# A fused long convolution and cosine-gated MLP: work at the changes of stage moved forward in the queues, and half of one stage's matrices made by ScalarE and GpSimd

## The chip, the cores and the metric

The kernel runs on one core of a Trainium2 chip. The core has five queues that matter here, each of which works strictly in its own order: TensorE (PE, matrix products; its weight loads are shown as PEld), VectorE (DVE), ScalarE (ACT), GpSimd (POOL), and SyncE (SP), which here issues all DMA transfers. They wait for each other by semaphores. The metric is the device time of one execution in microseconds (us); the number compared is the median of several executions. All data are 32-bit floats, and every matrix product is made in two passes over TensorE.

## What is computed

```python
def _attn_ref(x, v, pos_emb, w1, w2):            # x, v: (4, 12480, 128)
    B, S, D = x.shape
    h_mlp = np.maximum(pos_emb @ w1, 0.0) @ w2
    window = np.exp(-0.01 * np.arange(S, dtype=np.float32))[:, None]
    h_filt = h_mlp * window
    u = x * v
    L = 2 * S
    Uf = np.fft.rfft(u, n=L, axis=1)
    Hf = np.fft.rfft(h_filt, n=L, axis=0)
    y = np.fft.irfft(Uf * Hf[None, :, :], n=L, axis=1)[:, :S, :]
    return x * y

def _moe_ref(x, w_in, w_out):                    # x: (49920, 128), w_in: (128, 2048)
    h = x @ w_in
    return (h * np.cos(h)) @ w_out
```

Each of the 128 channels of x*v, in each of 4 batches, is convolved with a long filter that a small network makes from the positions; the product with x goes, row by row, through an MLP of width 2048 whose gate is a cosine. The MLP's weights arrive as 64-bit floats and are turned into 32-bit ones on the chip.

## The kernel before, in words

The convolution is done by a Fourier transform in two factors, N1 = 96 and N2 = 120, all by matrix products, in four steps for each batch:

- **First step** (f1_units, L576): for each of 64 columns of channels two products with the table c1 (f1_mm, L404). A bank of PSUM holds a column's result, and either ScalarE or VectorE copies it to SBUF (f1_evict, L417 to L424; f1_takers at L408 deals the columns out by a share).
- **Second step** (f2_both_units, L604, for batch 0): 48 pairs of frequencies. Each frequency needs a matrix w of 124x120 (make_w, L299, by turn, L282): a sine table times one number plus another times another. Each pair takes two products with the signal (L445) and two with the filter (L448; from the middle on as four at L451). ScalarE copies the filter's result to a tile h (L624), SP stores h to DRAM (hd, L626) and w to DRAM (wd, L613), since batches 1 to 3 load both again (f2_units, L585). VectorE multiplies signal and h (f2_product, L464), GpSimd adds the two halves (L471).
- **Third step** (i1_units, L631): again 64 columns, products with the table cs (i1_mm, L476), a copy of one half by ScalarE (L484), sum and difference by VectorE (L486).
- **Fourth step** (i2_units, L659): 30 groups; each group takes four matrices of cosines (a tile tm, made by make_group, L642, or loaded from td) and products with them (i2_mm, L501); VectorE multiplies by x (zs, L506).

The order is written out by hand. Every step is a Python generator; each yield is a place where another generator may put its instructions, and what is emitted first stands first in its engine's queue. The helper `units(n, steps, before, mm, after, parts, ahead)` (L524) is the frame of all steps: `before(j)` prepares unit j and is called `ahead` units early, `mm` emits the products, and `after(j)` takes the results out, one unit late.

For batch 0 the stages follow one another: the filter's network, the filter's first step (into ftile), batch 0's first step, second, third. While the filter's first step runs, GpSimd makes the remaining tables (inverse_tables, L252): every fifth yield advances them (L860 to L864), the sines themselves are taken by ScalarE (L226) up to four tables late, and what is left is emitted at once at the end. Into the first and the third step `beside` (L870) puts one piece of the conversion of w_in and w_out at every 14th yield (convert_units, L167: VectorE L133, L141, L151, GpSimd L135, L137, L147, L156, ScalarE L144 sig and L146 low), and in the third step, at every fifth of the others, one piece of the cosine matrices of six groups (some_groups, L653, through make_t, L305: two ScalarE instructions and one sum by GpSimd, L297). After them some_groups opens the fourth step of batch 0 (`next(backs[0])`, L657), which prepares its first group.

In the second step a matrix is made by one ScalarE multiplication into a bank of PSUM (L291) and one VectorE multiply-add (L293), one pair ahead and one being made; tiles w have two buffers, h three, t (L457) two. From the fourth step of batch 0 on, the convolution of the batches and the MLP (moe_up L734, moe_act L749, moe_down L756) are interleaved by counted steps, to the end.

Of the kernel before, what the change touches and what calls it, by code (L numbers as in the profile page):

```python
# [2 lines left out]

# [6 lines left out]
F32 = mybir.dt.float32  # L10
U32 = mybir.dt.uint32
AF = mybir.ActivationFunctionType
# [18 lines left out]
def kernel(  # L31
# [46 lines left out]
    nc = tc.nc  # L78
# [4 lines left out]
    N1, N2 = 96, 120  # L83
    R = S // N2
    M = N1 * N2
# [3 lines left out]
    KE = ODD + H  # L89
# [5 lines left out]
    CB = D // 2  # L95
# [156 lines left out]
    def inverse_tables(pool):  # L252

        t = Tables(pool, nc.gpsimd, 4)
        part = t.whole([P, 1], [[1, 1]], channel_multiplier=1, name="part")
        part4 = t.whole([P, 1], [[1, 1]], base=1, channel_multiplier=4, name="part4")
        step = t.whole([P, P], [[1, P]], name="step")
        mid = t.whole([P, P], [[1, P]], base=-MID, name="mid")
        cs, (rows, tw_t) = third_table(pool), last_tables(pool)
        yield from t.sines(step, part, N2, [(cs[:, 0, 0:H + 1], 1), (cs[:, 1, 0:H + 1], 0)],  # L260
                           eighths=slice(0, H + 1, H))
        yield from t.sines(step[:, 1:H], part, N2,
                           [(cs[:, 0, H + 1:], 0), (cs[:, 1, H + 1:], 1)])
        yield from t.sines(step, part4, 4 * N1,
                           [(rows[:, i, :], q) for i, q in enumerate((0, 1, 2, 3))])
        yield from t.sines(mid, part4, TURN, [(tw_t[:, 0, :], 1), (tw_t[:, 1, :], 0)],
                           eighths=slice(H - 1, N2, H))
        t.finish(len(t.waiting))
        for kept, made in ((csd, cs), (rowsd, rows), (twd, tw_t)):
            nc.sync.dma_start(kept[:, :, :], made[:, :, :])  # L270

# [27 lines left out]
    def make_w(w, k1, **how):  # L299


        turn(w, even[:, 0, :], even[:, 1, :], tw_w[:, 0, k1:k1 + 1], tw_w[:, 1, k1:k1 + 1],
             **how)
# [146 lines left out]
            for r, src in enumerate((ftile[0:KE, :, k, :], above[0:KE, :, k - KF, :])):  # L450
                nc.tensor.matmul(pi[:, r], w[:, i, :], src, start=True, stop=True)  # L451

    def f2_product(pool, ps, h, k1, whole):


        y = parts[0:N2, :, k1:k1 + 2, :, :].rearrange("p r k b i -> p r b (k i)")
        t = pool.tile([N2, 2, CB, 4], F32, name="t", bufs=1 + whole)  # L457
        uu = ps[0:N2, :].rearrange("p (r b j) -> p r b j", r=2, j=4)
        if whole:
            for r, (dst, hh) in enumerate(((y, h[:, :, :, :]), (t[:, :, :, :], h[:, ::-1, :, :]))):  # L460
                u = uu[:, r]
                twice = bass.AP(tensor=u.tensor, offset=u.offset,
                                ap=[u.ap[0], [0, 2], *u.ap[1:]])
                nc.vector.tensor_tensor(dst, twice, hh, op=ALU.mult)  # L464
                yield
        for r, op in ((0, ALU.subtract), (1, ALU.add)):
            if not whole:
                nc.vector.tensor_tensor(y[:, r], uu[:, 0], h[:, r], op=ALU.mult)
                yield
                nc.vector.tensor_tensor(t[:, r], uu[:, 1], h[:, 1 - r], op=ALU.mult)  # L470
            nc.gpsimd.tensor_tensor(y[:, r], y[:, r], t[:, r], op=op)  # L471
            yield

    def i1_mm(ps, b, i):
# [101 lines left out]
    def f1_units(bank, u, share=0.5, evict=f1_evict):  # L576
        def mm(j, ps, i):
            if i == 0:
                ps = bank()
            f1_mm(ps, u, j, i)  # L580
            return ps

        return units(CB, F1_STEPS, lambda j: None, mm, lambda j, ps: evict(ps, j, share), 2)
# [17 lines left out]
            yield from units(N1 // 2, F2_STEPS, before, mm,  # L601
                             lambda j, ps: f2_product(pool, ps, hs.pop(j), 2 * j, False), 4)

    def f2_both_units(bank):  # L604

        with tc.tile_pool(name="both", bufs=2) as pool:
            ws = {}

            def before(j):
                ws[j] = pool.tile([KE, 2, N2], F32, name="w")  # L610
                for i in range(2):
                    make_w(ws[j][:, i, :], 2 * j + i, half=bank)
                nc.sync.dma_start(wd[j, :, :, :], ws[j][:, :, :])  # L613

            def mm(j, ps, i):
                if i == 0:
                    ps = bank(), bank()
                for filt in range(2):
                    f2_mm(ps[filt], ws[j], 2 * j, i, filt=filt == 1)
                return ps  # L620

            def after(j, ps):
                h = pool.tile([N2, 2, CB, 4], F32, name="h", bufs=3)
                nc.scalar.activation(h[:, :, :, :].rearrange("p r b j -> p (r b j)"),  # L624
                                     ps[1][0:N2, :], AF.Copy, scale=1.0 / M)
                nc.sync.dma_start(hd[j, :, :, :, :], h[:, :, :, :])  # L626
                yield from f2_product(pool, ps[0], h, 2 * j, True)

            yield from units(N1 // 2, F2_STEPS, before, mm, after, 4, ahead=1)

    def i1_units(bank):  # L631
        with tc.tile_pool(name="mid", bufs=2) as pool:
# [20 lines left out]
    def some_groups(pool):  # L653
        for g in SOME:
            t = pool.tile([N1, G, 2, R], F32, name="some", bufs=2)
            yield from make_group(pool, g, t, G, bufs=2)
        next(backs[0])  # L657

    def i2_units(bank, b, bufs):  # L659

# [133 lines left out]
    with tc.manual_schedule():  # L794
        with tc.tile_pool(name="psum", bufs=8, space=PSUM) as psum, \
                ExitStack() as first:
            def bank():
                return psum.tile([P, BANK], F32, name="ps")
# [58 lines left out]
            keep.__exit__(None, None, None)  # L857
            with tc.tile_pool(name="tables", bufs=1) as pool:
                sines = inverse_tables(pool)
                for i, _ in enumerate(f1):  # L860
                    if i % 5 == 0:
                        next(sines, None)
                for _ in sines:
                    pass  # L864

            backs = [inverse_units(lambda: bank(), b) for b in range(B)]

            def beside(units, pieces, more=lambda pool: iter(())):  # L870
                with tc.tile_pool(name="convert", bufs=1) as pool:
                    convert, other = convert_units(pool, pieces), more(pool)
                    for i, _ in enumerate(units):
                        if i % 14 == 0:
                            next(convert, None)
                        elif i % 5 == 0:
                            next(other, None)
                    for _ in [*convert, *other]:
                        pass

            beside(f1_units(bank, slots[0:R, :, :, :], 0.55),
                   [(wind[:, c], w) for c, w in in_pieces])
            lpool = ctx.enter_context(tc.tile_pool(name="late", bufs=1))
            cs = third_table(lpool)
            nc.sync.dma_start(cs[:, :, :], csd[:, :, :])
            for _ in f2_both_units(bank):
                pass
            first.close()

# [97 lines left out]
```

## Time and profile before

| what | us |
|---|---|
| median of 7 executions | 3782.46 |
| lowest and highest | 3780.46 and 3784.91 |
| the profiled execution | 3780.46 |
| its span, first to last instruction | 3778.6 |
| TensorE busy | 3699.9 (98%) |
| VectorE busy | 2762.1 (73%) |
| GpSimd busy | 2590.5 (69%) |
| ScalarE busy | 2520.4 (67%) |
| mean granted TensorE clock | 0.994 |

Times in the profile count from the start of the span. A line of a stage table gives the stretch, its length, then for each engine its busy time and, in brackets, its number of instructions, then the granted clock of TensorE (1.00 is full), the busy share of the 16 DMA engines and GB/s. A line of waits names the waiting engine, tile and line, the one it waited for, and the time in total, how often and the longest. A line of the timeline gives start, duration, engine, line, operation, tiles (written <- read), shapes, how many instructions are merged, and in brackets the engine's idle time before and who ended it. SPq is SP's queue of DMA issues; the time shown is that of issuing, not of the transfer.

### The profile page before, as it was taken

What the parts mean: (1) busy time and instruction counts of PE and PEld (TensorE: products, weight loads), DVE (VectorE), ACT (ScalarE), POOL (GpSimd) and SP (SyncE); (2) the same over time, 40 slices, a digit from 0 to 9 for tenths busy, and PEclk for the clock granted to TensorE, in tenths of its full rate; (3) what the DMA queues carried; (4) which work ended last, traced back from release to release, by engine and by line L of the source; (5) the groups of instructions that cost most, each with busy time, mean ns of one, the idle gap of its engine ahead of it and who ended that gap; (6) DMA issues with size and microseconds to landing.
All of it is one profiled execution on the core that took longest, in us unless ns stands there. A gap on an engine that the chain in (4) does not pass through costs nothing.

```text
span 3778.6 us, 47199 instructions
## 1 busy us (share of the span) xinstructions
PE 3699.9 (98%) x13546; PEld 2108.4 (56%) x13546; DVE 2762.1 (73%) x5562; ACT 2520.4 (67%) x4683; POOL 2590.5 (69%) x2342
## 2 busy tenths in 40 slices
PE   7898999999999999999999999999999999999999
PEld 6777555655466555555565556555566544444444
DVE  7887887688866777778766786788765566666666
ACT  5757776766665557766655567666664677777777
POOL 7667886588854665688745664788644577777776
PEclk9899999999999999999999999999999999999999
DMA  6263441022202650122103540122105200000000
GB/s 166 67 181 109 149 148 54 19 72 78 74 18 68 181 156 27 35 76 79 57 18 111 176 123 21 48 79 75 41 12 168 87 22 18 17 21 19 17 22 13
DMA packets 209498, 276.14 MB, mean 73 GB/s; under 512 B 17111, under 2 KB 146535, under 8 KB 209111
## 3 DMA queue, kind: packets, MB, share of 16 engines
q1 hardware_dynamic: 209239, 273.12, 24.5%
q8 instruction: 109, 1.79, 0.2%
q14 instruction: 150, 1.23, 0.1%
HBM read 193.64 MB, written 79.42 MB: 72 GB/s over the span
## 4 chain that ended last, share of the span: by engine, by line
PE 83%; POOL 6%; DVE 3%; DMA 3%; ACT 2%; issue 2%; SPq 0%; POOLq 0%; DVEq 0%; ACTq 0%
PE ph L737 32%; PE acc L762 27%; PE cv L762 5%; PE cv L501 5%; PE cv L476 4%; POOL f L746 4%; PE cv L404 3%; PE cv L445 3%; PE ph L126 2%; DMA hd<-h 2%; PE ps L404 2%; DVE k L743 1%; ACT cs L751 1%; POOL tm L297 1%; PE ps L476 1%
## 5 line engine op out<-in xcount | busy, mean ns | idle before, releaser
L746 POOL TENSOR_TENSOR f<-a,k 128x512 f32<-128x512 f32 (+1 forms) x1568 | 1986.2, 1267 | 1050.5 <-DVE k L743 1050.2
L737 PE MATMUL ph<-at,w_in_sb 128*128 128x512 f32 (+1 forms) x3136 | 1599.0, 591 | 5.2 <-DVE gt L753 4.6
L740 ACT ACTIVATE a<-ph,quarter 128x512 f32<-128x512 f32 (+1 forms) x1568 | 1073.4, 685 | 756.6 <-PE ph L737 747.4
L762 PE MATMUL acc<-gt,w_out_sb 128*128 128x512 f32 (+1 forms) x2688 | 1374.3, 593 | 9.9 <-ACT ot L768 9.4
L753 DVE TENSOR_TENSOR gt<-ph,cs 128x512 f32<-128x512 f32 (+1 forms) x1568 | 1077.9, 687 | 317.7 <-ACT cs L751 289.3
L743 DVE TENSOR_SCALAR k<-a 128x512 f32<-128x512 f32 (+1 forms) x1568 | 769.9, 491 | 618.1 <-ACT a L740 601.7
L751 ACT ACTIVATE cs<-f 128x512 f32<-128x512 f32 (+1 forms) x1568 | 980.3, 625 | 330.3 <-POOL f L746 327.8
L762 PEld LDWEIGHTS acc<-gt,w_out_sb 128*128 128x128 f32 x2688 | 505.7, 189 | 662.7 <-issue 619.3
L737 PEld LDWEIGHTS ph<-at,w_in_sb 128*128 128x128 f32 x3136 | 553.6, 190 | 337.9 <-issue 264.6
L471 POOL TENSOR_TENSOR slots<-slots,t 120x256 f32<-120x256 f32 x384 | 311.1, 816 | 58.7 <-DVE t L464 26.2
L501 PEld LDWEIGHTS cv<-slots,tm 96*104 96x104 f32 x1920 | 240.1, 170 | 108.4 <-issue 80.7
L501 PE MATMUL cv<-slots,tm 96*104 96x128 f32 x1920 | 253.7, 274 | 9.7 <-DVE tm L293 4.9
L762 PE MATMUL cv<-gt,w_out_sb 128*128 128x512 f32 (+1 forms) x448 | 224.5, 583 | 0.7 <-DVE gt L753 0.7
L476 PEld LDWEIGHTS cv<-cs,slots 120*96 120x96 f32 x1536 | 176.7, 167 | 67.6 <-issue 65.7
L476 PE MATMUL cv<-cs,slots 120*96 120x120 f32 x1536 | 183.1, 266 | 0.0
L445 PE MATMUL cv<-slots,w 124*120 124x256 f32 x576 | 173.0, 380 | 0.0
L445 PEld LDWEIGHTS cv<-slots,w 124*120 124x120 f32 x576 | 103.6, 184 | 123.8 <-issue 111.1
L404 PEld LDWEIGHTS cv<-c,slots 104*124 104x124 f32 x768 | 132.5, 192 | 71.2 <-issue 58.3
L404 PE MATMUL cv<-c,slots 104*124 104x192 f32 x768 | 151.2, 326 | 4.8 <-DVE gt L753 3.5
L762 PEld LDWEIGHTS cv<-gt,w_out_sb 128*128 128x128 f32 x448 | 84.9, 190 | 104.5 <-issue 99.5
L392 DVE TENSOR_TENSOR xt<-xt,vt 104x256 f32<-104x256 f32 x177 | 138.1, 787 | 0.1
L486 DVE TENSOR_TENSOR slots<-cv,other 96x240 f32<-96x240 f32 x384 | 133.6, 394 | 4.2 <-ACT other L484 4.2
(129 smaller groups left out, 2565.5 us busy)
## 6 DMA issues: line engine op xcount, KB each, us to landing
h<-hd SPq DMA_DIRECT2D x144, 240.0 KB
tm<-td SPq DMA_DIRECT2D x96, 312.0 KB
xt<-in_x_dram SPq DMA_DIRECT2D x120, 208.0 KB
vt<-in_v_dram SPq DMA_DIRECT2D x120, 208.0 KB
xs<-in_x_dram SPq DMA_DIRECT2D x120, 208.0 KB
zd<-zs SPq DMA_DIRECT2D x119, 208.0 KB
zb<-zd SPq DMA_DIRECT2D x96, 256.0 KB
w<-wd SPq DMA_DIRECT2D x144, 116.2 KB
```

The costliest lines, as they stand in the source:

```text
L404: nc.tensor.matmul(ps[0:KE, i * 2 * N1:(i + 1) * 2 * N1], u[:, b, 0:KE, i], c1[0:u.shape[0], :, :].rearrange("p r k -> p (r k)"), start=Tr ...
L445: nc.tensor.matmul(pi, w[:, i, :], parts[0:KE, :, k], start=True, stop=True)
L471: nc.gpsimd.tensor_tensor(y[:, r], y[:, r], t[:, r], op=op)
L476: nc.tensor.matmul(ps[0:N1, (i * 2 + r) * N2:(i * 2 + r + 1) * N2], parts[0:N2, r, :, b, i], cs[:, r, :], start=True, stop=True)
L501: nc.tensor.matmul(ps[0:R, i * D:(i + 1) * D], t[:, i, r, :], slots[0:N1, :, place, :], start=(r == 0), stop=(r == 1))
L737: nc.tensor.matmul(ph[:, 0:m], w_in_sb[:, c * P:(c + 1) * P], ats[n][:, 0:m], start=True, stop=True)
L740: nc.scalar.activation(a[:, 0:m], ph[:, 0:m], AF.Identity, bias=quarter[:, 0:1], scale=INV_TWO_PI)
L743: nc.vector.tensor_scalar(out=k[:, 0:m], in0=a[:, 0:m], scalar1=ROUND, scalar2=ROUND, op0=ALU.add, op1=ALU.subtract)
L746: nc.gpsimd.tensor_tensor(f[:, 0:m], a[:, 0:m], k[:, 0:m], op=ALU.subtract)
L751: nc.scalar.activation(cs[:, 0:m], f[:, 0:m], AF.Sin, scale=TWO_PI)
L753: nc.vector.tensor_tensor(gt[:, 0:m], ph[:, 0:m], cs[:, 0:m], op=ALU.mult)
L762: nc.tensor.matmul(accs[n][:, 0:m], w_out_sb[:, c, :], gt[:, 0:m], start=(c == 0), stop=(c == NFC - 1))
```

## The change

It edits how batch 0's first three steps are put into the queues; the MLP part is untouched.

- inverse_tables yields between its last sines, and the generator that advances it goes on into batch 0's first step (`chain(f1, first_f1)`) instead of emitting the rest at once at the end of the filter's first step.
- f2_both_units prepares its first two pairs' matrices before batch 0's first step goes on (`next(f2)`), in buffers of their own (w_pool), and each later pair two ahead. Of a pair's two matrices the odd one is now made by ScalarE twice and a GpSimd sum (the `spare` way of turn, L295 to L297); the even one as before. Matrices have three buffers (two in w_pool, one in the step's pool), h has two. A pair's store wd is issued after the store hd of the pair before it in work, not when it is made.
- The last pair's two sums at the end of f2_product go to VectorE.
- `beside` puts conversions at every 11th yield in the first step and every 10th in the third, and the other work at yields 1, 5, 9 and so on.
- some_groups opens the fourth step before its last group, not after it.

```diff
         yield from t.sines(mid, part4, TURN, [(tw_t[:, 0, :], 1), (tw_t[:, 1, :], 0)],
                            eighths=slice(H - 1, N2, H))
-        t.finish(len(t.waiting))
+        while t.waiting:
+            t.finish(1)
+            yield
...
-    def f2_product(pool, ps, h, k1, whole):
+    def f2_product(pool, ps, h, k1, whole, sums=nc.gpsimd):
...
-            nc.gpsimd.tensor_tensor(y[:, r], y[:, r], t[:, r], op=op)
+            sums.tensor_tensor(y[:, r], y[:, r], t[:, r], op=op)
...
-    def f2_both_units(bank):
-
+    def f2_both_units(bank, w_pool):
+
+        ws, unkept = {}, []
+
+        def before(j):
+            ws[j] = (w_pool if j % 3 < 2 else pool).tile([KE, 2, N2], F32, name="w",
+                                                         bufs=2 if j % 3 < 2 else 1)
+            spare = (w_pool if j < 2 else pool).tile([KE, N2], F32, name="spare",
+                                                     bufs=1 if j < 2 else 2)
+            make_w(ws[j][:, 1, :], 2 * j + 1, spare=spare[:, :])
+            yield
+            make_w(ws[j][:, 0, :], 2 * j, half=bank)
+            unkept.append(j)
+            yield
+
+        def mm(j, ps, i):
+            if i == 0:
+                ps = bank(), bank()
+            for filt in range(2):
+                f2_mm(ps[filt], ws[j], 2 * j, i, filt=filt == 1)
+            return ps
+
+        def after(j, ps):
+            h = pool.tile([N2, 2, CB, 4], F32, name="h")
+            nc.scalar.activation(h[:, :, :, :].rearrange("p r b j -> p (r b j)"),
+                                 ps[1][0:N2, :], AF.Copy, scale=1.0 / M)
+            nc.sync.dma_start(hd[j, :, :, :, :], h[:, :, :, :])
+            while unkept:
+                k = unkept.pop(0)
+                nc.sync.dma_start(wd[k, :, :, :], ws[k][:, :, :])
+            yield from f2_product(pool, ps[0], h, 2 * j, True,
+                                  nc.vector if 2 * j + 2 == N1 else nc.gpsimd)
+
+        steps = units(N1 // 2, F2_STEPS, before, mm, after, 4)
+        yield next(steps)
         with tc.tile_pool(name="both", bufs=2) as pool:
-            ws = {}
-
-            def before(j):
-                ws[j] = pool.tile([KE, 2, N2], F32, name="w")
-                for i in range(2):
-                    make_w(ws[j][:, i, :], 2 * j + i, half=bank)
-                nc.sync.dma_start(wd[j, :, :, :], ws[j][:, :, :])
...
-                h = pool.tile([N2, 2, CB, 4], F32, name="h", bufs=3)
...
-            yield from units(N1 // 2, F2_STEPS, before, mm, after, 4, ahead=1)
+            yield from steps
...
             yield from make_group(pool, g, t, G, bufs=2)
-        next(backs[0])
+            if g == SOME[-2]:
+                next(backs[0])
...
-                for i, _ in enumerate(f1):
-                    if i % 5 == 0:
-                        next(sines, None)
-                for _ in sines:
-                    pass
+                first_f1 = f1_units(bank, slots[0:R, :, :, :], 0.55)
+                for i, _ in enumerate(chain(f1, first_f1)):
+                    if i % 5 == 0 and next(sines, "made") == "made":
+                        break
...
-            def beside(units, pieces, more=lambda pool: iter(())):
+            def beside(units, pieces, every, more=lambda pool: iter(())):
...
-                        if i % 14 == 0:
+                        if i % every == 0:
                             next(convert, None)
-                        elif i % 5 == 0:
+                        elif i % 4 == 1:
                             next(other, None)
...
-            beside(f1_units(bank, slots[0:R, :, :, :], 0.55),
-                   [(wind[:, c], w) for c, w in in_pieces])
+            w_pool = first.enter_context(tc.tile_pool(name="w", bufs=2, side="right"))
+            f2 = f2_both_units(bank, w_pool)
+            next(f2)
+            beside(first_f1, [(wind[:, c], w) for c, w in in_pieces], 11)
...
-            for _ in f2_both_units(bank):
+            for _ in f2:
                 pass
...
-            beside(i1_units(bank), [(w_out_sb[:, c, :], w) for c, w in out_pieces], some_groups)
+            beside(i1_units(bank), [(w_out_sb[:, c, :], w) for c, w in out_pieces], 10, some_groups)
```

More of the change, by code (lines that the diff above doesn't have):

```diff
@@ L2 @@
 from contextlib import ExitStack
+from itertools import chain
 import concourse.bass as bass
@@ L602, in f2_units @@
                              lambda j, ps: f2_product(pool, ps, hs.pop(j), 2 * j, False), 4)
-    def f2_both_units(bank):
-        with tc.tile_pool(name="both", bufs=2) as pool:
-            ws = {}
-            def before(j):
-                ws[j] = pool.tile([KE, 2, N2], F32, name="w")
-                for i in range(2):
-                    make_w(ws[j][:, i, :], 2 * j + i, half=bank)
[L613 to L622, printed above, removed]
-                h = pool.tile([N2, 2, CB, 4], F32, name="h", bufs=3)
[L624 to L627, printed above, removed]
-            yield from units(N1 // 2, F2_STEPS, before, mm, after, 4, ahead=1)
+    def f2_both_units(bank, w_pool):
[28 more added lines that the diff above has]
+        yield next(steps)
+        with tc.tile_pool(name="both", bufs=2) as pool:
+            yield from steps
```

## The prediction, made before the result was known

> **What bounds the kernel now.** I read the chain of work that ended last, then the whole span cut at the changes of stage, then who TensorE waits for. From the page:
>
> ```profile
> PE 83%; POOL 6%; DVE 3%; DMA 3%; ACT 2%; issue 2%; SPq 0%; POOLq 0%; DVEq 0%; ACTq 0%
> ```
>
> Stages cut where TensorE resumes (time, busy time of each engine, granted clock, DMA share, GB/s):
>
> ```profile
> 120.93:170.17 49.24, 44.38 (x252) 43.48 (x253) 40.35 (x110) 43.42 (x130) 29.45 (x32) 0.92 0.23 67
> 170.17:272.13 101.96, 96.57 (x483) 74.90 (x483) 85.56 (x191) 53.79 (x142) 68.00 (x96) 0.98 0.59 173
> 272.13:336.95 64.82, 55.58 (x510) 54.32 (x510) 50.08 (x155) 43.04 (x133) 44.58 (x58) 0.95 0.25 80
> 336.95:3778.60 3441.65, 3410.97 (x11856) 1861.47 (x11856) 2490.28 (x4806) 2313.90 (x4050) 2359.23 (x2012) 1.00 0.23 68
> ```
>
> The last row, 91% of the span, is full of TensorE work and the change does not touch its order: it only moves its start. So the question is when the fourth step begins. TensorE's waits before 345 us:
>
> ```profile
> PE ps L404 <- ACT slots L412: 7.5, 3, 7.1
> ...
> PE ps L445 <- DVE w L293: 6.3, 4, 4.7
> PE cv L501 <- DVE tm L293: 4.9, 1, 4.9
> ...
> PE ps L476 <- POOL slots L471: 3.3, 2, 3.1
> ```
>
> These four waits (longest: 7.1, 4.7, 4.9, 3.1) are what the change aims at: 20 us, plus the half clock granted after each (0.50 in 120.93 to 126.25 and in 170.17 to 174.04). A wait removed counts only down to what is late next, so I go stage by stage. All sums are against the profiled execution: 3780.46 us (span 3778.6 and 1.9 around it), 2.0 below the median of 3782.46, which I add at the end.
>
> **First step.** Before, TensorE sits from 113.87 to 120.93: its next bank is freed by a ScalarE copy queued behind both tw_t sines, which wait for GpSimd (117.21, 119.41). After, that copy stands ahead of them and ends near 115.6. TensorE then runs three columns (half clock) and needs the bank of a copy whose last parts are queued behind tw_t and six new ScalarE instructions for the first two matrices: 119.73 + 0.47 + 6 x 0.30 (the six at L291 took 1.78) + 0.6 = 122.6. Before, the same column began at 124.92, so 2.3 us are gained there; about 1.2 are left once the clock is full again, as the new gap also brings a half clock. From 128 on ScalarE is the bound: evictions 1.05 us apart and pairs of conversions of 0.77, one gap of 1.4, until 169.38, while TensorE is done at 165.48. After: 122.6 + 34 x 1.05 + 8 x 0.77 = 164.5, plus the early waits for TensorE (about 2.2) and 0.8 for conversions: 167.5. Denser conversions (every 11 pieces, not 14) leave this sum as it is. The matrices, ready, save the 0.8 from 169.38 to 170.17. TensorE starts the second step at 167.55: **-2.6** (bounds -1.0 and -3.6, by no and by both ScalarE gaps). The 4.7 us wait mostly remains, now on evictions.
>
> **Second step.** Who waits, and the store queue:
>
> ```profile
> 186.65 0.60 ACT L624 ACTIVATE h<-ps 120x512 f32<-120x512 f32 x1 [1.01 <-DMA hd<-h]
> 186.67 0.24 SPq L613 DMA_DIRECT2D wd<-w  x1
> ...
> 187.00 0.32 SPq L626 DMA_DIRECT2D hd<-h  x1
> ...
> 188.66 0.60 ACT L624 ACTIVATE h<-ps 120x512 f32<-120x512 f32 x1 [0.88 <-DMA hd<-h]
> 188.68 0.24 SPq L613 DMA_DIRECT2D wd<-w  x1
> ...
> 189.02 0.36 SPq L626 DMA_DIRECT2D hd<-h  x1
> ```
>
> Stores of a pair are issued every 2.01 us, TensorE needs 1.74 (four lines of two passes, 0.435 apart), VectorE 1.9 (0.59 + 0.6 + 0.68). The landings (the trace's updates of the transfers' counts) are 2.00 to 2.02 apart from the first pair on, though the first issues are only 1.8 to 1.9 apart and latency grows from 3.18 to 4.0: a saturated server. The last three hd stores, with no wd between, land 0.62 apart; so hd costs 0.62 and wd, with half the bytes, 1.39. wd 0 and 1, issued 0.54 apart, land 1.50 apart, which agrees. The change touches neither store. The matrices themselves become cheaper (VectorE loses 48 x 0.30; GpSimd gains 48 sums, between 0.43 for 96x120 and 0.62 for 96x208, I take 0.44 as 120 elements is nearest), but GpSimd's pair is then 1.42 + 0.44 = 1.86 and hides under 2.01; at 0.62 it would show as 0.03 x 48 = 1.6. ScalarE: 0.6 + 3 x 0.3 = 1.5, hidden too.
>
> [...]
>
> What does change is the order. Before, wd 0 and 1 left in idle time (170.35, 170.89) and three h buffers let the last ScalarE copy wait for hd 44, after 45 hd and 45 wd from 174.62 on. After, SP issues hd 0 first (at 172.15: 167.55 plus 4.6, as 170.17 to 174.91 now) and wd 0, 1, 2 behind it; with two h buffers the last copy waits for hd 45, after 46 hd and 47 wd: +0.62 + 2 x 1.39 = **+3.4**. hd starts moving 1.90 after issue (2.52 alone, less 0.62), wd 1.44 (2.83 - 1.39): **+0.5**. The first store of the unbroken row is issued at 172.15, not 174.62: **-2.5**, which is the first step's gain passed on. A wait is added: ScalarE's first term of matrix j+3 takes the buffer of j and waits for store wd j, 1.39 after hd j-2 lands; behind it in ScalarE's queue stands the h copy of the next pair, for which VectorE's product and the next hd store wait. ScalarE's pair then ends 0.40 late in each turn, which the row of stores still hides. At its end two VectorE sums (0.33 each from 96x240, at most 0.68 from 120x512) take the place of GpSimd's 1.4: **-0.75** (at most; -0.05). The third step starts at 272.8, not 272.13.
>
> **Third step.** Here VectorE and ScalarE bound each other, not TensorE:
>
> ```profile
> DVE slots L486 <- ACT other L484: 14.7, 24, 1.3
> ACT sig L144 <- DVE sig L141: 12.9, 8, 2.0
> ```
>
> Conversions come every 6.93 us with 14 evictions (0.33 each) between: ScalarE's sig waits until VectorE has worked off its evictions, then VectorE waits 1.06 for the next copy. Reckoned instruction by instruction along these two queues, now comes to 6.8. After, 10 evictions stand between conversions and a table piece (0.735 on ScalarE) every two columns, not 2.5: 5.15 and 5.45 in turn, and GpSimd needs 5.3 for each (1.16 + 1.15 + 0.72 + 0.75 + 2.5 x 0.61). Before: first sig 280.45, seven cycles and 7.4 to the last eviction, 336.55. After: rows and tw_t are loaded once hd 47 has landed (273.15, now 272.10), so the first conversion's data come 1.05 later; ScalarE's queue now begins with a table piece that waits for that load, so four columns are done by then, not six. 281.5 + 4 x 5.15 + 3 x 5.45, 2% to 4% more, = 319.6; then 25 columns, with tm for the first fourth-step group (six ScalarE instructions of 0.37, GpSimd between) in the queue: 21.8. 341.4 instead of 336.55: **+4.2** beyond the late start. tm being ready saves only 336.55 to 336.95, less 0.1: **-0.3**; the rest of that 4.9 us wait is for evictions, TensorE's clock is cold either way, and sixteen cold passes (0.207 each) and the eviction to zs at 340.73 follow as now.
>
> Sum: -2.5 + 3.4 + 0.5 - 0.75 + 4.2 - 0.3 = +4.5: 3785.0 for the profiled execution, **3787.0** for the median.
>
> **Rivals.** (1) The stalls really go: stores do not hold the pairs, which run at GpSimd's 1.86 (48 x -0.15 = -7), the first step gives -2.6, the end of the second -0.75, nothing is lost later: 3772. For it: 0.59 DMA share and 1.74 on TensorE. Against: landings 2.01 apart even behind a short queue. (2) **Two h buffers** become the bound, the slower side: hd lands, ScalarE's copy starts 0.40 later (held by the matrix before it), hd is issued 0.65 after that, then comes its latency. At 2.01 a pair there is room for a latency of 2.96; it decides above that. If it stays at the 3.59 of the steady stage now, a pair takes (3.59 + 1.05)/2 = 2.32, 46 x 0.31 = +14: 3801. For it: 3.59 in nearly all pairs. Against: that latency is queueing, the last store had 2.52. (3) The third step does not lose: VectorE catches up once conversions are over, so +4.2 is 0: 3782.8, the change moves waits and does nothing it says. For it: VectorE and ScalarE are busy 50 and 43 of 65 us.
>
> **How the numbers follow.** A measurement of this kernel can tell about 0.2% (7.6 us) from no change: 3774.9 to 3790.0. Forecast 0.45, of which a quarter above 3790 (GpSimd at 0.62, a late first step); rival 1 0.15; rival 2 0.18; rival 3 0.22. Faster 0.15; slower 0.18 + 0.11 = 0.29; same 0.56. The range must reach to both outer rivals: 3771 to 3800.
>
> **What would show it.** Right: second-step hd issues 2.0 apart, ScalarE's h waiting for hd; TensorE in it from about 167.6 to 272; VectorE's last L486 near 341; cold clock at the fourth step. Wrong: hd issues 1.9 apart (rival 1) or over 2.2 (rival 2); last eviction before 338 (rival 3); or anything but a shift after 350.

## The result and the profile after

| | before | after |
|---|---|---|
| median, us | 3782.72 (33 runs) | 3793.74 (13 runs) |
| lowest and highest | 3778.94 and 3786.80 | 3790.73 and 3799.29 |
| profiled execution, its span | 3780.46, 3778.6 | 3799.29, 3797.5 |

The ratio is 1.0030 (95% interval 1.0022 to 1.0037): slower by 11 us (8 to 14). The range of the prediction, 3771 to 3800, held it, but that range is wide and reaches to both sides of no change. The sign was right; the size, +4.5, was 6.5 short. By the prediction's own measure, in which less than 7.6 us counts as no change, this is a slower kernel, to which it gave 0.29. The profiled execution of after happens to be the slowest of its 13, so I use it to see *where* time went and count *how much* over the profiles of all kernels that share a stage.

The chain of the work that ended last, shares of the span by engine, on the page of after:

```profile
PE 80%; POOL 7%; DVE 4%; DMA 4%; ACT 3%; issue 2%; SPq 0%; POOLq 0%; DVEq 0%; ACTq 0%
```

TensorE's share fell from 83% to 80%; GpSimd, VectorE, ScalarE and DMA each gained a point. The stages of after, cut where TensorE resumes (stretch, length, busy time of PE, PEld, DVE, ACT, POOL, granted clock, DMA share, GB/s):

```profile
123.86:172.19 48.33, 44.03 (x241) 41.95 (x241) 40.99 (x108) 40.54 (x119) 31.23 (x32) 0.92 0.23 68
172.19:279.88 107.69, 97.53 (x480) 75.03 (x481) 77.61 (x144) 68.10 (x186) 85.07 (x140) 0.97 0.56 164
279.88:353.54 73.66, 61.36 (x513) 59.68 (x513) 53.97 (x157) 45.48 (x137) 47.06 (x60) 0.91 0.27 84
353.54:3797.50 3443.96, 3410.22 (x11856) 1858.75 (x11856) 2490.92 (x4805) 2311.85 (x4046) 2358.07 (x2010) 1.00 0.23 68
```

The second step grew by 5.7 us and the third by 8.8 (before: 101.96 and 64.82); counted from first product to first product, as below, by 6.4 and 8.2. TensorE's work is not the reason: it was busy 97.5 against 96.6 in the second, and the 5.8 it gained in the third come with a lower clock (0.91, not 0.95) and lie beside the waits shown next. Between these two profiles 16.6 of the 18.9 us are lost before the fourth step starts, as forecast. And the waits, of the stretch up to 365 us:

```profile
ACT w L294 <- DMA wd<-w: 30.6, 42, 4.7
...
PE ps L479 <- DVE slots L489: 11.0, 7, 2.7
...
PE ps L407 <- ACT slots L415: 7.6, 5, 4.7
...
ACT some L294 <- DMA tw_t<-twd: 6.4, 1, 6.4
...
PE ps L448 <- DVE w L296: 5.4, 8, 2.2
...
ACT h L631 <- DMA hd<-h: 3.9, 5, 1.6
```

Of the four gaps that the change aims at three shrank: TensorE now pauses for 1.78 and 4.73 where it paused for 7.06, for 2.92 before the second step (4.69) and for 1.33 before the fourth (4.88). The one before the third step grew from 3.06 to 3.92. New waits stand inside the stages: ScalarE waits 42 times for the store of a matrix (first row), and TensorE 11.0 us in the middle of the third step for VectorE's evictions (second row). The 6.4 us in which ScalarE waits for its tables, with evictions queued behind, are new too.

### The profile page after: what moved, and what is told of

Same layout as the page of the kernel before. It is cut to its first block, busy times and chain, and to the rows that moved or that the text cites. A ratio compares the mean times of both kernels' runs of the same rounds, so it can differ in the third digit from the quotient of the medians.

```text
span 3797.5 us, 47301 instructions
## 1 busy us (share of the span) xinstructions
PE 3709.1 (98%) x13546; PEld 2112.5 (56%) x13546; DVE 2763.6 (73%) x5516; ACT 2536.2 (67%) x4731; POOL 2612.2 (69%) x2388
## 4 chain that ended last, share of the span: by engine, by line
PE 80%; POOL 7%; DVE 4%; DMA 4%; ACT 3%; issue 2%; SPq 0%; POOLq 0%; DVEq 0%; ACTq 0%
PE ph L752 31%; PE acc L777 26%; PE cv L777 5%; PE cv L504 4%; PE cv L479 4%; POOL f L761 4%; PE cv L407 3%; PE cv L448 3%; PE ph L127 2%; DMA wd<-w 2%; DMA tm<-td 1%; ACT cs L766 1%; POOL tm L300 1%; DVE k L758 1%; PE ps L407 1%
## 5 line engine op out<-in xcount | busy, mean ns | idle before, releaser
L474 POOL TENSOR_TENSOR slots<-slots,t 120x256 f32<-120x256 f32 x382 | 310.1, 818 | 22.3 <-DVE t L473 16.6
```

The lines of the kernel that those rows point to most:

```text
L474: sums.tensor_tensor(y[:, r], y[:, r], t[:, r], op=op)
```

## Experiments

Each kernel was compared with the kernel before on the same chip, where that one's median was 3784 to 3786 (in the first row 3783), so ratios are compared and not times. A stage counts from its first product to the next stage's first product; for the kernel before that makes the second step 101.28 and the third 65.50.

| kernel | ratio to before (95%) | second step | third step |
|---|---|---|---|
| after | 1.0030 (1.0022 to 1.0037) | 107.70 | 73.65 |
| third step, two edits undone | 1.0022 (1.0013 to 1.0031) | 106.25 | 68.40 |
| third step wholly undone | 1.0016 (1.0007 to 1.0024) | 106.39 | 65.36 |
| third step, conversions alone | a single run: 3797.5 | 107.19 | 73.00 |
| third step, tables alone | a single run: 3792.9 | 107.84 | 66.57 |
| first step's cadence undone | 1.0027 (1.0018 to 1.0036) | 107.38 | 75.17 |
| first two wd early | 1.0023 (1.0014 to 1.0032) | 104.69 | 74.99 |
| every wd ahead of hd | 1.0019 (1.0009 to 1.0028) | 102.97 | 71.85 |
| before, two buffers of h | 1.0014 (1.0004 to 1.0024) | 104.47 | 65.86 |
| after, wd split | 0.9980 (0.9971 to 0.9990) | 89.96 | 71.87 |
| before, wd split | 0.9973 (0.9964 to 0.9982) | 89.22 | 65.32 |
| combination | 0.9971 (0.9960 to 0.9982) | 90.97 | 65.53 |
| combination, matrices on VectorE | 0.9971 (0.9959 to 0.9982) | 89.40 | 65.29 |

My theory was that each stage keeps its own bound (the row of stores in the second step, VectorE and ScalarE holding each other in the third) and that the edits crowd these bounds. The rival was that the new order brings waits of its own, above all through two buffers of h.

### The third step

Two of its three edits put back:

```diff
-            def beside(units, pieces, every, more=lambda pool: iter(())):
+            def beside(units, pieces, every, more=lambda pool: iter(()), cycle=4, place=1):
...
-                        elif i % 4 == 1:
+                        elif i % cycle == place:
...
-            beside(i1_units(bank), [(w_out_sb[:, c, :], w) for c, w in out_pieces], 10, some_groups)
+            beside(i1_units(bank), [(w_out_sb[:, c, :], w) for c, w in out_pieces], 14, some_groups, 5, 0)
```

> The changed kernel with one thing put back: in the third step conversions stand at every 14th yield and table pieces at every fifth of the others, as before the change. Theory A (crowding): the third step loses because conversions and table pieces come closer than VectorE, ScalarE and GpSimd can work them off; between the first and the last conversion they stood 5.35 and 6.70 apart in turn after the change, for 10 evictions, against 6.93 for 14 before. Then the third step falls from 73.7 us to 64.8 to 66.5, conversions are 6.9 apart again, and the median falls by 7 to 9, to about 3785. Rival B (late start): the third step loses by its tables' late loads and by the first fourth-step group opened early, both of which stay; then it stays above 72 and the median within 2 us of 3793.7.

The stretch from the third step's first product to the fourth's:

```profile
275.42:343.82 68.40, 57.22 (x513) 55.41 (x513) 50.69 (x157) 45.04 (x138) 46.00 (x60) 0.93 0.27 83
```

5.3 to 6.8 of the loss are gone, more than rival B allows and less than theory A said. Seven conversions are again 6.64 to 7.70 apart, but the last stands 9.70 after the one before it. Between these two lie the six ScalarE terms of the fourth step's first group. So the third edit was put back too:

```diff
-            if g == SOME[-2]:
-                next(backs[0])
+        next(backs[0])
```

> The changed kernel with the whole third step put back as before the change: conversions at every 14th yield, table pieces at every fifth of the others, and the fourth step opened after the last table group, not before it. With only the first two put back the step took 68.4 us, against 73.7 to 75.2 in three profiles with the change and 65.5 before it. Theory A: the rest is the early opening, whose six ScalarE terms held the last conversion (9.7 us after the one before it, where 6.9 is usual); then the step takes 65.3 to 66.3, and the median is 2 to 3 below that of the run with two parts put back. Rival B: the rest is the later load of the tables; then it still takes 67.5 to 68.5.

The third step of this kernel:

```profile
275.53:340.89 65.36, 55.92 (x513) 54.55 (x513) 50.20 (x156) 42.95 (x133) 44.59 (x59) 0.95 0.26 80
```

Theory A: the early opening by itself cost 3.0 in this kernel. Over all kernels here the third step then falls into two clear groups: 65.3 to 65.9 with its old code (six profiles, mean 65.5), 71.9 to 75.2 with the new (five, mean 73.5).

The medians follow in part only: the ratio goes from 1.0030 to 1.0022 and 1.0016, some 3 and 5 us with intervals that overlap, where the step got 5.3 and 8.3 shorter. The rest comes back later: from the fourth step's first product to the end these two kernels take 3446.1 and 3446.7, after 3444.0 (see "Fourth step" below).

Then conversions and table pieces each alone, with the opening last. First the conversions at every 10th yield, with the same two new arguments of `beside`:

```diff
-            beside(i1_units(bank), [(w_out_sb[:, c, :], w) for c, w in out_pieces], 10, some_groups)
+            beside(i1_units(bank), [(w_out_sb[:, c, :], w) for c, w in out_pieces], 10, some_groups, 5, 4)
```

> The changed kernel with the third step as before the change but for the conversions, which stay at every 10th yield (table pieces one in five, opening last). It tells conversions from table pieces. The step took 65.4 with all put back and 73.7 to 75.2 with the change. Theory A (VectorE and GpSimd disturb each other): with the change every second conversion's VectorE operation took 1.39, not 0.28, while GpSimd's sums of table pieces ran in front of its product, and conversions were 5.35 and 6.7 apart; with one table piece each 2.5 columns at fixed places the same meets every conversion or none: spacings all 6.5 to 6.8 (step 74 to 77) or all 5.2 to 5.4 (67.5 to 69.5). Rival B (conversions are not what costs): 65 to 66.5.

Conversions alone cost 7.6 (73.00), so rival B falls; spacings are 6.14 to 6.20, all alike as theory A says, but between its two figures. Timeline of this kernel, one conversion (start, duration, engine, line, operation):

```profile
316.41 0.80 POOL L300 TENSOR_TENSOR some<-some,spare 96x208 f32<-96x208 f32 x1 [0.84 <-ACT spare L299]
316.65 1.40 DVE L134 TENSOR_SCALAR power<-raw 128x256 uint32<-128x256 uint32 x1
...
317.18 0.72 POOL L157 TENSOR_TENSOR w_out_sb<-sig,power 128x256 f32<-128x256 f32 x1
...
317.97 0.28 DVE L142 TENSOR_SCALAR sig<-raw 128x256 uint32<-128x256 uint32 x1
...
318.34 0.42 ACT L145 ACTIVATE sig<-sig 128x256 f32<-128x256 uint32 x1 [2.01 <-DVE sig L142]
```

VectorE's L134, mostly 0.28, begins while GpSimd is in a sum, lasts through GpSimd's product as well and ends 0.15 after it. ScalarE's sig waits behind that (2.01), and the evictions' copies behind sig. The same in after, for every second conversion:

```profile
297.99 2.37 POOL L300 TENSOR_TENSOR some<-some,spare 96x208 f32<-96x208 f32 x3
...
299.79 1.39 DVE L142 TENSOR_SCALAR sig<-raw 128x256 uint32<-128x256 uint32 x1
300.32 0.72 POOL L157 TENSOR_TENSOR w_out_sb<-sig,power 128x256 f32<-128x256 f32 x1
...
301.22 0.42 ACT L145 ACTIVATE sig<-sig 128x256 f32<-128x256 uint32 x1 [2.10 <-DVE sig L142]
```

Here conversions are 5.32 to 5.38 apart where L142 takes 0.28 and 6.68 to 6.76 where it takes 1.39. Of the eight conversions one VectorE operation was so stretched in the old third step, three in the new one and seven in this kernel. I did not try the same conversions with GpSimd's operations moved elsewhere, so that GpSimd's operations hold VectorE's is inferred from these times, not shown.

Last, table pieces alone at yields 1, 5, 9:

```diff
-            beside(i1_units(bank), [(w_out_sb[:, c, :], w) for c, w in out_pieces], 10, some_groups)
+            beside(i1_units(bank), [(w_out_sb[:, c, :], w) for c, w in out_pieces], 14, some_groups, 4, 1)
```

> The changed kernel with the third step as before the change but for the table pieces, which stay at yields 1, 5, 9 and so on (conversions every 14th, opening last). Theory A: the first piece stands ahead of the first eviction and waits for its tables, so evictions start 4 to 4.5 later than with all put back; TensorE has free banks for most of that, and one more piece every second cycle costs ScalarE 0.4 a cycle: the step takes 67 to 69.5. Rival B (table pieces cost nothing, they end earlier instead): 65 to 66.

66.57, 1.2 more than with all put back: below theory A, above rival B. The first conversion comes 10.42 after the step's start, not 8.9; VectorE and ScalarE make up most of the late evictions. The three edits do not add up: alone they cost 7.6, 1.2 and (with the old cadence) 3.0, together 8.3. So the conversions carry most of the loss; what the early opening costs beside dense conversions no run shows.

### The first step

```diff
-            beside(first_f1, [(wind[:, c], w) for c, w in in_pieces], 11)
+            beside(first_f1, [(wind[:, c], w) for c, w in in_pieces], 14)
```

> The changed kernel with conversions in the first step at every 14th yield, as before the change, and nothing else put back. Theory A (crowding): ScalarE waits for VectorE at conversions for 3.0 us in the first step after the change and 1.4 before; the step's last ScalarE eviction comes 1.5 to 2.2 earlier relative to the first conversion's, the second step starts as much earlier, and the median falls by 1.5 to 2.2. Rival B: the late start of the second step (172.19, not 170.17) comes from the tables' last sines and the six new ScalarE instructions alone; then the median moves by less than 0.7.

ScalarE's waits at conversions fell from 3.0 to 2.0 us, and from the last tw_t sine to the second step it took 50.3, against 49.8 to 51.2 in eight profiles with the denser cadence. So for this profile rival B's "less than 0.7" holds; but the two combinations below, with the same cadence, took 49.2 and 49.6, so a gain of up to 1 us is not excluded. The ratio cannot tell either way. A surprise sits ahead of it: that sine, which waits for GpSimd's tables in every kernel, ended anywhere between 118.4 and 121.9 us in the fourteen profiles, old code and new, and the second step's start moves with it. Counted from it, the first step takes 50.6 in three profiles of the old code and 50.35 in the eight.

### The second step: order and buffers

The first two matrices stored when made:

```diff
-            unkept.append(j)
+            if j < 2:
+                nc.sync.dma_start(wd[j, :, :, :], ws[j][:, :, :])
+            else:
+                unkept.append(j)
```

> The changed kernel, but the matrices of the first two pairs are stored when they are made, before the first step goes on, not behind the first store of h. Theory A (a saturated row of stores): the two leave the row, 2 x 1.38, and the 4.7 us wait of ScalarE for the store of matrix 0, with the 2.2 us of TensorE behind it, is gone; from first h store to last the stage is 3 to 4 shorter, and the median falls by 3 to 4. Rival B (two buffers of h bound the pairs, not the row): the pairs stay as they are behind the first three, and only the start's hole of 0.8 + 0.7 in the landings goes; the median falls by 1.5 or less.

What it removes, in the timeline of after:

```profile
176.62 0.34 SPq L633 DMA_DIRECT2D hd<-h  x1
...
177.00 1.36 SPq L636 DMA_DIRECT2D wd<-w  x3
...
181.33 0.39 ACT L294 ACTIVATE w<-even,tw_w 124x120 f32<-124x120 f32 x1 [4.74 <-DMA wd<-w]
...
182.20 0.57 ACT L631 ACTIVATE h<-ps 120x512 f32<-120x512 f32 x1
...
182.68 0.70 PE L448 MATMUL ps<-slots,w 124*120 124x256 f32 x2 [2.18 <-DVE w L296]
...
182.80 0.32 SPq L633 DMA_DIRECT2D hd<-h  x1
```

The second hd is issued 6.2 us after the first: ScalarE's next matrix needs the buffer that wd 0 is stored from, the next copy of h stands behind it, and hd 1 comes when the row of stores has stood idle for 0.6 (wd 2 landed at 184.08, and hd 1, issued at 182.80, can start to move 1.90 later by the estimate of the prediction). Another 0.8 is missing before wd 0 lands, though it was issued in time. With the two stores early the step takes 104.69, against a mean of 107.1 in six profiles of the changed order: 2.4 less, between the two theories. Then every wd as soon as it is made, ahead of hd, still with two buffers of h:

```diff
-            unkept.append(j)
+            nc.sync.dma_start(wd[j, :, :, :], ws[j][:, :, :])
...
-            while unkept:
-                k = unkept.pop(0)
-                nc.sync.dma_start(wd[k, :, :, :], ws[k][:, :, :])
```

> The changed kernel, but every pair's matrices are stored when they are made, so wd of pair j+2 stands ahead of hd of pair j, as before the change; two buffers of h as in the changed kernel. It puts the slower rival of the prediction to its test: with wd ahead, hd took 3.59 from issue to landing before the change, and with two buffers of h that would hold a pair at (3.59 + 1.05)/2 = 2.32. Theory A (the row of stores is the bound, latency is queueing): with a buffer less, fewer stores queue, hd's latency falls to about 3 and h stores stay 2.0 to 2.05 apart; the first two wd leave the row, so the stage takes 103 to 105.5, and the median falls by 1 to 4. Rival B (two h buffers bind): 2.2 to 2.35 apart, the stage 9 to 15 longer than the changed kernel's 107.

102.97, 4.1 less, a shade under theory A's span; rival B is out: hd issues are 2.01 apart at the median, 2.08 in the mean. The same question put to the kernel before:

```diff
-                h = pool.tile([N2, 2, CB, 4], F32, name="h", bufs=3)
+                h = pool.tile([N2, 2, CB, 4], F32, name="h", bufs=2)
```

> The kernel before the change with two buffers of h, not three, and nothing else. Theory A: the row of stores stays the bound, 2.01 apart; the last copy of h waits for hd 45, not hd 44, so the third step starts one pair's stores (0.64 + 1.38 = 2.0) later, and the median rises by 1.5 to 2.5. Rival B (two buffers bind): h stores 2.1 to 2.35 apart, the second step 5 to 15 longer.

SP's queue in this kernel:

```profile
242.94 0.24 SPq L613 DMA_DIRECT2D wd<-w  x1
243.27 0.38 SPq L626 DMA_DIRECT2D hd<-h  x1
244.96 0.24 SPq L613 DMA_DIRECT2D wd<-w  x1
245.29 0.38 SPq L626 DMA_DIRECT2D hd<-h  x1
```

The spacing stays 2.02 at the median (2.08 in the mean, 2.01 before) and the latency of hd falls from 3.59 to 3.2, which agrees with the prediction's "that latency is queueing". Still the step is 3.2 longer than before (104.47), 1.2 more than the 2.0 expected. The holes in the row that no late issue explains (last section) add up to 2.7 here and 1.6 before, about as much. A third buffer of h in the changed kernel was not tried.

### The second step: the cost of a store

In the trace of before the count of a store of 124 rows has one early step and 4 late ones (wd 2: 175.03, then 177.28 to 177.45), that of a store of 120 rows one early and 15 late ones (hd 0: 175.43, then 177.36 to 178.09).

```diff
-                nc.sync.dma_start(wd[k, :, :, :], ws[k][:, :, :])
+                nc.sync.dma_start(wd[k, 0:112, :, :], ws[k][0:112, :, :])
+                nc.sync.dma_start(wd[k, 112:KE, :, :], ws[k][112:KE, :, :])
```

> The changed kernel, but each store of matrices is two transfers, of 112 and of 12 rows, in place of one of 124. Theory A: a store of 124 rows takes 1.38 of the row because its count ends in only 4 late steps, each for 31 rows; divided into 16 and 12 parts it takes about as long per byte as the store of h (0.64 for 240 KB, so 0.31 to 0.5 for 116 KB), a pair's stores take 0.95 to 1.2, and GpSimd's 1.9 a pair becomes the bound: h stores 1.85 to 1.95 apart, the stage 4 to 8 shorter, median 4 to 8 less. Rival B: the row is bound by bytes written and not by the number of parts; then h stores stay 2.01 apart, or more with one transfer more, and the median is the same within 1.

SP's queue in this kernel, and then its second step:

```profile
207.47 0.32 SPq L633 DMA_DIRECT2D hd<-h  x1
207.89 0.33 SPq L636 DMA_DIRECT2D wd<-w  x1
208.28 0.39 SPq L637 DMA_DIRECT2D wd<-w  x1
209.34 0.32 SPq L633 DMA_DIRECT2D hd<-h  x1
```

```profile
170.88:260.84 89.96, 85.49 (x480) 73.24 (x481) 73.66 (x144) 66.54 (x186) 83.18 (x140) 1.00 0.70 196
```

The same bytes in one transfer more, and the step is 17 shorter: twice what theory A asked for. hd issues are 1.70 apart at the median and 1.82 on average, the latency of hd is back at 2.5, and both parts of a wd have landed 0.37 (median) after the hd before them, where a whole one cost 1.39. Their counts end in 16 and 12 late steps, that of the whole store in 4. So it was not its bytes that made wd expensive; the cheaper stores are those with more late steps. What a step stands for no trace shows: theory A's 31 rows are 124 / 4, an estimate of mine. That two transfers in place of one help by themselves was not tested apart; against it, wd 0 and wd 1 before the change, two transfers of 4 late steps each, landed 1.50 apart. Is that the changed kernel's affair alone? The kernel before, with the same two lines in place of its one:

> The kernel before the change with nothing of the change, but with each store of matrices as two transfers of 112 and of 12 rows. The changed kernel's second step fell from 107.7 to 90.0 us by this alone. Theory A (the row of stores bounds the second step of both kernels): here VectorE is next, 0.60 + 0.60 + 0.68 = 1.88 a pair, so h stores are 1.85 to 1.9 apart and not 2.01, the step falls from 101.3 to 93 to 96, and the median by 5 to 8. Rival B: with wd ahead of hd and three buffers of h the stores were hidden here, and the gain belongs to the changed kernel's waits alone; then the median is the same within 1.5.

The second step of this kernel:

```profile
171.66:260.88 89.22, 86.35 (x480) 74.68 (x481) 82.54 (x191) 53.73 (x142) 67.52 (x96) 0.98 0.70 198
```

12 shorter; rival B is out. VectorE was not next at 1.88, as I thought: hd issues are 1.70 apart at the median, and TensorE is busy for 86.35 of 89.22. All that seemed good together, and the same with the matrices back on VectorE:

> The changed kernel with the split stores of matrices, the first two matrices stored when made, conversions at every 14th yield in both steps, and the third step wholly as before. If the parts add up: the split kernel's 0.9980 of the kernel before, less 6 us in the third step, less 0 to 2 for the first two stores (the row no longer bounds), less 0 to 2 in the first step: 0.9953 to 0.9965 of the kernel before, about 3770 beside 3785. If the third step's bound is met again by some other way (it starts nearer to the load of its tables): 0.997 to 0.998.

> The same as the run before it, but with both matrices of a pair made by one ScalarE term and one VectorE multiply-add, as before the change, and none by GpSimd; two pairs ahead as in the changed kernel. It tells what the change's half of the matrices on ScalarE and GpSimd is worth where the stores no longer bound. Theory A: VectorE has 0.60 + 0.60 + 0.66 = 1.86 to 1.9 a pair against 1.55, GpSimd 1.4 against 1.86; pairs were 1.82 apart on average with the split stores, so the stage is 2 to 4 longer than in the run before it. Rival B: TensorE's 1.74 and ScalarE bound both; the same within 1.

```diff
-            spare = (w_pool if j < 2 else pool).tile([KE, N2], F32, name="spare",
-                                                     bufs=1 if j < 2 else 2)
-            make_w(ws[j][:, 1, :], 2 * j + 1, spare=spare[:, :])
+            make_w(ws[j][:, 1, :], 2 * j + 1, half=bank)
```

The second step of the combination, and then of the same with matrices on VectorE:

```profile
167.57:258.54 90.97, 87.71 (x480) 75.36 (x481) 73.79 (x144) 66.60 (x186) 83.40 (x140) 0.97 0.69 194
```

```profile
171.46:260.87 89.41, 86.84 (x481) 74.78 (x481) 82.59 (x190) 53.32 (x140) 66.63 (x94) 0.97 0.71 197
```

The combination reaches 0.9971: its interval touches what the parts should give, but the value itself lies in the other case's 0.997 to 0.998. Its third step did become short (65.53); from the fourth step on it takes 3448.5, the longest of all, where the split alone in the changed kernel takes 3441.8. It cannot be told from the split alone in the kernel before (0.9973). Both beat both kernels; I saw nothing left of the change that beats the two lines of the split. GpSimd's half of the matrices is worth nothing here: VectorE does them too, 82.59 busy of 89.41, in a step that is 1.6 shorter, which neither theory said. With stores out of the way TensorE, 96 to 97% busy, is the nearest bound with either.

## Why the prediction was right in sign and short in size

**What bounds it**: right. Nearly everything was decided before the fourth step's start, and each stage's own bound was what mattered.

**First step, -2.6**: wrong by 2.4; it is -0.25 over eight profiles. The early columns came 1.3 earlier (123.84 against 125.16 for ScalarE's second copy, with tables 1.3 later, so 2.6 for the like), but TensorE, at half clock behind its new gap (0.50 from 123.86 to 130.23), then made ScalarE wait 1.96 and 1.53, where I had allowed 2.2 in all, and conversions cost 3.0 (2.4 to 2.5 in the other profiles) where I had 0.8.

**Second step, +3.4, +0.5 and -0.75**: the row of stores as bound holds, the size was 2.6 short. The step is 107.1 in the mean, +5.8 against the one profile of before, where the three terms make +3.2. Two buffers of h, one hd and one wd more ahead of the last copy, cost 3.2 in the kernel before, not 2.0. The new order of the stores (4.1 by the kernel with every wd ahead) had 1.9 of me, one more wd and 0.5: the added wait of ScalarE for wd, which I said the row would hide, is not hidden at the start, where it lets the row stand idle for 0.6. The rest is of the size of the holes in the row (4 to 5 us in all, 1.6 before, last section); what causes them stays open. And the sign I had named, ScalarE's h waiting for hd, came 5 times only (3.9 us): it waited for wd instead (42 times, 30.6). The last sums on VectorE gave 0.4 to 1.0: from the last store's issue it was 2.21 to the third step's first product and 2.89 to where products go on, now 1.85. Kernel by kernel: 101.28 before, +3.2 with two buffers, -1.5 with every wd ahead (the sums and the rest of the change), +4.1 by the new order. That the row saturates at 2.01 a pair, and that a store of 124 rows costs 1.38 to 1.39 and one of 120 rows 0.62 to 0.64, was right; with the split the bytes of wd have landed 0.37 after the hd before them. The counts have 4 late steps for 124 rows, 15 for 120, 16 and 12 for 112 and 12.

**Third step, +4.2**: the step that failed most, as "5.15 and 5.45 in turn". Conversions came 5.35 and 6.70 apart in all five profiles, 1.45 more for each two: 41.6 us over the seven spacings, where I had 36.95 and 2% to 4% more, 38.1. That is 3.5 of the 3.8 by which the term was too small (mean loss 8.0). I had taken VectorE's 0.28 for granted beside GpSimd; three of the eight conversions held one of 1.39.

**Fourth step, -0.3**: "TensorE's clock is cold either way" was wrong. The first products of the fourth step, before and after:

```profile
336.95 4.97 PE L501 MATMUL cv<-slots,tm 96*104 96x128 f32 x24 [4.88 <-DVE tm L293]
```

```profile
353.54 2.89 PE L504 MATMUL cv<-slots,tm 96*104 96x128 f32 x24 [1.33 <-DVE slots L489]
```

With the conversions done early TensorE runs without a pause from 337.2 to the end of the third step, pauses 1.33 and keeps its clock (1.00 from 353.54 to 356.50; before, 0.50 from 336.95 to 341.29): 24 passes in 2.89, not 4.97 (2.88 or 2.89 in all five kernels with the new third step, 4.73 to 5.45 in the six with the old). That is 2 us. From here to the end the new third step takes 3441.5 to 3444.0 and the old one 3441.7 to 3448.5: 2.8 less in the mean, though both spread. So the fourth step's term was short by 2.5, to the other side.

Together: -0.25 + 5.8 + 8.0 - 2.8 = 10.8, beside a measured 11. That the parts meet the whole so closely is in part luck: the second step's share rests on one profile of before, and the old kernels' time behind the fourth step's start spreads by 7 us.

**Rivals.** (1) fell on its premise, the stores do hold the pairs; 3772 was reached only when the store itself was made cheaper. (2), 3801, missed the time by about as much to the other side, and by the wrong mechanism: pairs stayed at 2.01 to 2.02 at the median with two buffers, in three kernels. (3) fell: the third step loses most of all. The 0.56 for no visible change rested on terms that nearly cancel; three of them erred to the slower side, by 2.4, 2.6 and 3.8, and one by 2.5 to the faster.

## What to carry to other kernels

Moving what an engine waits for to the front of a queue shortens that wait; whether the stage gets shorter is set by the stage's own bound, and if the moved work shares that bound it gets longer. Find the resource first: here a store of half the bytes cost twice as much (1.39 against 0.62), and splitting it 112 and 12 was worth 10 us in the one kernel and 19 in the other. Denser side work was not free here though each engine's sum of durations said that it would fit: an operation of 0.28 in the stretch that the sum was taken from took 1.39 in three of the eight conversions of the crowded one.

## What the runs showed of the hardware that was not expected

- A VectorE operation of 0.28 (in the conversions) took 1.39 or 1.40 where it began under one GpSimd operation and the next began before that one had ended: in before at 300.37, in after at 299.79, 311.85 and 323.91, with conversions alone at 316.65. Where the next began 0.08 after the end, in the first step of after (142.26, 150.99, 159.77), it took 0.82 and ended 0.15 after the first. Where it ran in 0.28 under a sum of table pieces (after, 299.59), that sum took 1.01, mostly 0.62. What decides which of the two goes first the traces do not show.
- The row of stores has holes of 0.3 to 1.0 that no missing issue explains (a landing later than the landing before it plus 0.62 or 1.39), 4 to 5 in all in four profiles of the changed order and 1.6 before, mostly at the same places (wd 19, hd 24, hd 35, wd 39, wd 47); several, not all, stand within 2 us of an instruction load of 8 or 16 KB in the DMA records (after: wd 19 landed at 220.65, a load of 8 KB began at 219.40). What causes them stays open.
- Pauses of TensorE of 1.33 and 1.78 (after) left the clock at 1.00 in the 3 us behind them; one of 1.59 (before, at 95.77) was followed by 0.51 from 98.90 to 102.40, one of 4.88 by 0.57 from 336.95 to 342.00. So in these two profiles the length of the pause alone does not decide it. Where it lies goes with it: between 60 and 365 us the stretches of one clock in them (before 98.94 to 102.36 and 167.21 to 174.04 at 0.50, for instance) are all whole multiples of 3.413 us long. Cut into steps of that length, the two profiles have 11 steps at full clock in which TensorE's pauses over 0.3 took 0.47 of the time or more, each followed by one at half clock; of four with 0.39 to 0.42 one was, of those with 0.37 or less none. The 1.59 lay within one step (0.47 of it); the 1.78 was cut by a boundary, and the 1.33 fills 0.39. What sets the clock the traces do not show.
